# The opening of a fused LayerNorm, long-convolution and FFN kernel: warming products, tap products, the first weight load and early FFN blocks put in another order

## The chip, the cores and the metric

The kernel runs on one core of a Trainium2 chip. The metric is the device time of one execution in microseconds, as a median over several runs. Engines are named as in the profile: PE (TensorE matmuls; PEld its weight loads), DVE (VectorE), ACT (ScalarE), POOL (GpSimd), SP (SyncE, which issues most DMAs).

## The reference

```python
x = A_q                                   # 1 x 2048 x 640, bf16
xn = layernorm(x)
# branch s: a short causal convolution of k (4 taps), times v, then a convolution over all 2048 positions
k_shift = sum(k_pad[:, t:t + S, :] * shift_k[:, 3 - t] for t in range(4))
kv = k_shift * v
y = irfft(rfft(kv_pad) * rfft(ssm_k_pad))[:S] + kv * ssm_D
s = xn * y
# branch g: a feed-forward network, F = 1728
g = silu(gelu(xn @ w1 + b1) @ w2 + b2)
return x + s * g
```

## The kernel before, in words

Position p*16+j of the sequence lies in partition p, row j. The sixteen rows j are cut into four chunks of four (`xn_tiles`). The FFN takes one chunk (512 positions) at a time in transposed form: step `h` with number 14*c+ft multiplies 128 columns of `w1` (block ft of 14) with the five transposed tiles `xT` of chunk c, five products of 128x512 into one PSUM bank, and `he` takes the bank through Gelu on ACT (L400). `g` is the second product (28 half rows). The long convolution is a two-stage Fourier transform by matmuls: first stages `kf` (of the kernel) and `uf` (of the signal) with the matrices `WA` and `WB` (L351), small stages with 32x32 blocks, and their inverses. `WA` and `WB` are made in the kernel: DVE forms the integer phases (step `w`, L249), and ACT takes a Sin (`ws0`, L253), an Abs (`ws1`, L256), a second Sin (`ws2`, L258) and a small Sin (`ss`, L309). PSUM has eight banks, and `banks[:, b]` is one of them.

The order of the work is written out by hand: `prologue()` first, and then the text `PLAN`, whose entries name a step, its number, the engine of its copy (`.a` ACT, `.d` DVE, for stores `.s` SP and `.p` POOL) and, after `@`, the PSUM bank or the row slots in SBUF. Every engine and every DMA queue works through its own instructions in this order, and waits where an operand is not there or a bank or slot is still in use.

What `prologue()` does for chunk 0, in its order on each engine:

- SP: rows 0, 1 and 2-3 of chunk 0 (L665, three DMAs), then `w1` columns 0 to 640 (`load_w1(0)`, L208), and from `PLAN` the rest of `w1` (`A1`), `C0` and so on. `C0` to `C4` load `ssm_k` into rows 0 to 15 of `rows`; the four tap weights `skp` lie in row 12 to 15, in partition 0, until they are used.
- PE: `warm(6)`, six products of a zeroed 128x512 tile `blank` (L637); the tap products (`w_exp_matmuls`, L318), eight products of one row of ones with 320 strided elements, which spread the four taps over all partitions; the transposes of rows 0 and 1 (`turn(0)`, L646); `feed(ft, 0)` for ft = 0 to 4, the first 256 positions of five FFN blocks (25 products of 128x256, L391); the transposes of rows 2 and 3 (`turn(2)`); `feed(ft, 1)`, the second 256 positions of the five blocks (25 products); then `h9`, `pt` (a transpose of the biases), `h12`, `h7`, `h11` from `PLAN`.
- DVE: memsets, the integer product (L245), the statistics of the rows (L616, L619), the reciprocal (L625), the normalisation (L628), three of five copies of each `turn` (L153), and then `w`, the small phases `s`, statistics of the later chunks, and `pb`, which copies the biases out of PSUM (L529, L530).
- ACT: a Sqrt for the table (L668), two copies of zeros into `kh` (L674, L675), the roots (L622), the copies of the taps out of PSUM (`taps_out`, L640), two of five copies of each `turn` (L152), a Gelu for the table (L703), and then `ws0`, `ws1`, `ws2`, `ss` and the `he` of `PLAN`.

Blocks 0 to 4 lie in banks 0 to 4, `h9` in bank 5, the transposes and later `pt` and `h7` in bank 6, `h12` in bank 7; `h11` takes bank 1 after `he1`. `h5` stands in `PLAN` after `he8`.

Of the kernel before, what the change touches and what calls it, by code (L numbers as in the profile page):

```python
# [11 lines left out]
BF16 = mybir.dt.bfloat16  # L12
# [15 lines left out]
WARM0, WARM1 = 6, 0  # L28
EARLY = 5
# [9 lines left out]
ie2.a@98 kc5.d@100 kc12.a@101 kc4.d@102 kf3@2 ke3.a@104 lv1 lr1 cv0@106 cv5@16 he13 cv13@18 kt10@4 kf10@6 ln8
q3@20 ln11 ke10.a@22 g0@5 kf11@2 ge0@0 kf13@0 kf9@6 ke11.a ke13.a@24 kc10.d@103 ke9.a@26 g3@4 ln4 ge3@1 kf2@2  # L40
cv11@28 ln5 kf7@0 ke7.a ln6 ln7 tt6@5 V1@30 te6.a@32 tt5@6 tt7@7 te7.a@33 ks3.p cv3@34 kt13@4 kc13.a@73 ks5.s
te5.a@59 cv2 ln9 cv4 cv6 gm3 ke2.a ks1.p g6@0 kf12@4 ke12.a tt8@1 te8.a@60 ge6@2 kf8@6 cv7 cv25@62 kt15@2
kc15.a@61 cv9@76 ke8.a kt9@3 kc9.a@100 uf1@4 ue1.a@22 cv8@34 cv10 g2@1 ge2@3 uf3@6 q7@16 ue3.a@90 tt9@0 cv17@96
kf1@2 ks6.p ke1.a@104 uf0@4 g1@1 ue0.a cv12 cv14 V3@76 ln10 kf14@6 te9.a@80 ge1@1 ke14.a@28 kf0@2 ke0.a ks0.p
kt8@4 cv16@24 kc8.a@82 gm2 cv15 ks2.s V2@18 q1@88 cv21@30 kt11@5 kf15@0 kc11.a@75 V4@0 V6@2 ke15.a uf2@6 g7@2
ks7.p ue2.a V5@4 ks4.s fl4@6 uf7@3 ge7@3 tt11@5 te11.a@102 gm6 tt13@0 te13.a@85 uf6@6 ue6.a@8 ue7.a tt10@1
te10.a@92 g5@2 kf16@6 cv19@10 cv18 cv20 cv22 ge5@2 cv23 tt14@5 te14.a@12 uf5@3 uf11@0 ue5.a@14 ue11.a@106 g4@2
gm0 ke16.a@96 cv32@104 cv24@10 ge4@0 uf10@4 ue10.a h14@3 cv29@30 tt12@0 us3.p cv26 cv27@18 uf4@6 he14@13 uf9@1
gm5 fl0@28 cv28 h23@4 gm4 fl6@26 cv30 te12.d@72 h21@5 cv31 us1.p ue9.a@68 ue4.a uf14@0 he23@74 fl1@64 uf12@2
ue14.a@66 cv41@62 us2.s uf8@6 ue8.a cv37@8 ue12.a@34 h17@4 he17@81 uf15@0 ue15.a cv33@18 uf13@6 us7.s he21@83  # L50
tt19@2 te19.a@84 cv35@30 h18@3 ue13.d ff0@0+6 fe1.a@76 us4.s cv40@24 cv42 h22@4 cv43@90 us5.p he18@93 fl2@10
fe0.a kf24@6 h20@5 ke24.a@14 ff1@2+0 fe3.a@36 fe2.a cv57@38 cv34 cv53@106 h16@6 fl3@28 he16@94 kf17@0 ke17.a
h26@7 cv45@62 us6.p kf18@2 he22@66 h24@6 ke18.a@68 cv36 he20@67 cv38 ff2@0+2 cv39 fe4.a@64 cv48@18 fe5.a us0.p
cv49@40 mk0@42 ml0@30 he24@44 mk1@34 h19@4 cv50 uf16@0 h25@5 ue16.a@8 cv51@22 kf23@2 he19@82 ml1@10 he26@56
ke23.a@0 cv52 cv54 kf22@0 ke22.a mk2@40 ml4@46 ks8.p h15@6 he15@75 cv44 he25@45 ml2@22 h27@4 mu0@2+0 mp1@106
V7@32 mp0@30 he27 g8@7 ge8@2 gm8 kf19@5 ke19.a cv46 uf19@0 g9@4 ue19.a@90 cv55 fl5@96 mu1@2+6 ml6@42 kf25@0
ke25.a q0@76 mp3@62 ge9@0 g10@5 ge10@2 mc0@0+6 me1.a@10 mp2@2 fl7@100 kf28@4 ke28.a@30 ks11.p ks9.s me0.d ks12.p
kf20@2 ke20.d@106 uf17@6 ff3@0+4 ue17.a cv47 us8.s mu2@2+6 mp4@34 fe7.a@36 fe6.a ms0.s mk3@28 kf21@4 ke21.a
mp5@22 gm10 kf27@0 uf27@4 ke27.a@4 ue27.a@0 ff4@2+0 fe8.a@68 fe9.a ml3@14 cv59@6 ff5@4+6 fe11.a@40 fe10.a g11@2
ml7@64 ge11@2 gm9 ff6@0+6 fe13.a@8 cv56@96 cv58 fe12.d mk4@52 mc1@4+2 me3.d@10 me2.a kf29@6 ke29.a tt18@0 ks14.s  # L60
tt16@1 mk6@54 te18.d@59 mc2@4+2 me4.a@26 kf26@6 g12@0 ke26.a ks13.s mk5@38 cv60 ml5@2 cv61@62 cv62 gm11
te16.a@60 me5.a cv63 uf18@4 mu3@6+2 ge12@0 ue18.a g13@1 mp6@22 ge13@2 kf31@4 ke31.a@34 mp7@6 uf25@6 ue25.a@48
kf30@0 ke30.d mc3@2+4 me6.a@50 us9.p ks15.p ks10.s fl15@62 me7.d uf29@6 ue29.a@30 fl8@14 ms1.p uf20@0 ue20.d@104
uf22@2 fl9@32 ue22.a@4 uf30@4 ue30.a@28 uf23@6 ue23.a gm7 uf24@0 ue24.d tt15@2 h30@3 he30@80 us12.p gm13 fl10@36
te15.d@103 gm1 mu4@4+0 uf21@6 mp9@6 ue21.a mp8@22 g15@2 ge15@3 fl11@90 mu5@0+6 ms3.s g14@3 mp10@34 mp11@106
# [26 lines left out]
def kernel(  # L92
# [514 lines left out]
    def prologue():  # L607
# [23 lines left out]
        blank = rows[:, WE0, 0:4 * P]  # L631
        tp_of = [banks_b[:, 6 + t // 3, t % 3 * 2 * P:(t % 3 + 1) * 2 * P] for t in range(DT)]
        pw = banks[:, 7, :]

        def warm(n):
            for _ in range(n):
                nc.tensor.matmul(out=pw, lhsT=blank[:, 0:P], rhs=blank, start=True, stop=True)  # L637
# [19 lines left out]
        nc.vector.memset(blank, 0.0)  # L657
# [52 lines left out]
        for ft in range(EARLY):  # L710
            feed(ft, 1)
# [49 lines left out]
```

## Time and profile before

| | |
|---|---|
| median of 3 runs | 211.58 us (209.90, 212.39, 211.58) |
| the profiled execution | 212.68 us, of which the span of its instructions is 210.9 us |
| PE busy | 195.6 us (93%), 2176 matmuls |
| DVE busy | 175.9 us (83%) |
| ACT busy | 155.0 us (74%) |
| chain that ended last | PE 77%, ACT 10%, DMA 6% |
| DMA | 57.72 MB, mean 274 GB/s |

The profile is one execution of the program. Its times count from the first instruction of the span. A timeline row reads: start, busy time, engine, line, operation, output and input tiles with their shape, count, and in brackets the idle time of the engine before it and what ended it. A row can merge several instructions of one kind. PE rows include the time in which a product runs through the array; the distance of two starts is what one product costs in a row of them.

### The profile page before, as it was taken

The page shows a single profiled execution, that of the slowest core. Times are in us where ns is not written, and L with a number is a line of the kernel's source. Part 1 is how long each engine was busy: PE and PEld are TensorE (multiplying, and loading weights), DVE is VectorE, ACT ScalarE, POOL GpSimd, SP SyncE. Part 2 cuts the span into 40 slices and gives each one's busy share as a digit, 9 for nine tenths or more (in the row PEclk, how much of TensorE's full clock was granted, in tenths as well). Part 3 has the DMA queues.
Part 4 walks back from the last instruction along what each step waited for, and adds up shares of the span by engine and source line. Part 5 has one row for each costly group of instructions (what it writes and reads, how often), then busy time and mean ns, then how long its engine had stood idle before and what let it go on. Part 6 is the DMA issues. An engine that isn't in the chain of part 4 may idle for free.

```text
span 210.9 us, 5483 instructions
## 1 busy us (share of the span) xinstructions
PE 195.6 (93%) x2176; PEld 114.8 (54%) x2192; DVE 175.9 (83%) x307; ACT 155.0 (74%) x247; POOL 30.9 (15%) x55
## 2 busy tenths in 40 slices
PE   7698499999999999998899999999999989999992
PEld 2365157778776544563565644456655434357771
DVE  8829789999899999999999977762999888753894
ACT  6839959999999999969969899594144976753110
POOL 8100010403022021110012203100010100330330
PEclk9769859999999999999999999999999999999999
DMA  6999999715879899998868896757997678569963
GB/s 167 391 420 348 356 365 371 265 38 185 262 221 352 266 330 320 297 328 303 290 256 296 248 343 212 273 174 226 303 387 258 201 234 266 178 229 281 367 229 113
DMA packets 46876, 57.72 MB, mean 274 GB/s; under 512 B 3009, under 2 KB 36594, under 8 KB 46850
## 3 DMA queue, kind: packets, MB, share of 16 engines
q1 hardware_dynamic: 44016, 47.36, 68.6%
q0 software_dynamic: 2832, 10.00, 13.1%
q8 instruction: 17, 0.28, 0.5%
q14 instruction: 9, 0.07, 0.1%
q10 hardware_dynamic: 2, 0.01, 0.0%
HBM read 33.76 MB, written 18.35 MB: 247 GB/s over the span
## 4 chain that ended last, share of the span: by engine, by line
PE 77%; ACT 10%; DMA 6%; issue 3%; SPq 1%; DVE 1%; ACTq 0%
PE banks L391 28%; PE banks L413 26%; PE banks L351 8%; ACT rows L152 5%; PE banks L495 4%; PE banks L584 3%; DMA w_sb<-in_B_w_dram 3%; DMA rows<-rows 3%; PE banks L442 3%; PE banks L560 3%; PE banks L382 2%; PE banks L513 1%; ACT WB L253 1%; ACT WA L258 1%; ACT rows L256 1%
## 5 line engine op out<-in xcount | busy, mean ns | idle before, releaser
L391 PE MATMUL banks<-rows,w_sb 128*128 128x512 bf16 (+1 forms) x289 | 70.4, 382 | 7.3 <-ACT rows L400 1.9
L152 ACT CAST rows<-banks 128x640 bf16<-128x640 f32 x105 | 69.9, 720 | 4.0 <-PE banks L495 1.7
L413 PE MATMUL banks<-w_sb,rows 128*128 128x320 bf16 x416 | 61.7, 299 | 0.0
L549 DVE TENSOR_TENSOR rows<-banks,rows 128x1280 bf16<-128x1280 f32 x32 | 46.1, 1484 | 3.7 <-PE banks L495 2.5
L413 PEld LDWEIGHTS <-rows 128*128 128x128 bf16 x416 | 39.8, 98 | 16.8 <-issue 0.2
L391 PEld LDWEIGHTS <-w_sb 128*128 128x128 bf16 x305 | 29.6, 103 | 34.4 <-issue 8.3
L400 ACT ACTIVATE rows<-banks,b_f 128x512 bf16<-128x512 f32 x52 | 35.0, 704 | 9.8 <-PE banks L391 9.6
L418 ACT ACTIVATE sl_all<-banks 128x320 bf16<-128x320 f32 x32 | 14.5, 458 | 30.7 <-PE banks L413 28.5
L480 DVE TENSOR_TENSOR rows<-rows 128x1280 bf16<-128x1280 bf16 x32 | 26.1, 822 | 0.5
L476 DVE TENSOR_TENSOR rows<-rows 128x1280 bf16<-128x1280 bf16 x32 | 25.2, 820 | 0.8 <-DMA scrK<-rows 0.8
L153 DVE CAST rows<-banks 128x640 bf16<-128x640 f32 x23 | 18.6, 821 | 7.2 <-PE banks L560 3.9
L152 ACT COPY rows<-banks 128x512 bf16<-128x512 bf16 (+3 forms) x27 | 17.4, 695 | 4.0 <-PE banks L646 4.0
L351 PE MATMUL banks<-rows,WA 128*128 128x320 bf16 x64 | 18.7, 299 | 0.9 <-ACT rows L152 0.6
L351 PE MATMUL banks<-rows,WB 128*128 128x320 bf16 x64 | 18.7, 298 | 0.0
L423 DVE TENSOR_TENSOR xn<-xn,sl_all 128x320 bf16<-128x320 bf16 x32 | 10.0, 319 | 8.2 <-ACT sl_all L418 8.0
L495 PE MATMUL banks<-rows,mats 32*32 32x320 bf16 x512 | 12.9, 304 | 0.6 <-ACT rows L152 0.3
L596 DVE TENSOR_TENSOR rows<-banks,xn 128x640 bf16<-128x640 f32 x12 | 9.6, 819 | 2.8 <-PE banks L584 2.8
L495 PEld LDWEIGHTS <-mats 32*32 32x32 bf16 x512 | 5.2, 87 | 12.4 <-issue 10.7
L153 DVE COPY rows<-banks 128x640 bf16<-128x640 bf16 (+3 forms) x18 | 6.9, 411 | 4.8 <-PE banks L646 4.0
L584 PE MATMUL banks<-rows 128*128 128x320 bf16 x64 | 10.6, 299 | 0.1
L568 POOL DMA_DIRECT2D scrC<-rows x7 | 5.3, 764 | 36.5 <-ACT rows L152 28.0
L458 POOL DMA_DIRECT2D scrK<-rows x9 | 5.0, 553 | 36.4 <-ACT rows L152 32.2
(95 smaller groups left out, 182.2 us busy)
## 6 DMA issues: line engine op xcount, KB each, us to landing
rows<-scrK SPq DMA_DIRECT2D x16, 320.0 KB, 5.4
rows<-rows SPq DMA_DIRECT2D x32, 160.0 KB, 3.4
rows<-scrU SPq DMA_DIRECT2D x16, 320.0 KB, 5.0
rows<-scrC SPq DMA_DIRECT2D x16, 320.0 KB, 5.4
scrU<-rows POOLq DMA_DIRECT2D x10, 320.0 KB, 4.1
scrK<-rows POOLq DMA_DIRECT2D x9, 320.0 KB, 4.6
scrC<-rows SPq DMA_DIRECT2D x9, 320.0 KB, 3.5
rows<-in_A_ssm_k_dram SPq DMA_DIRECT2D x5, 512.0 KB, 11.9
```

The source lines that it names most:

```text
L152: return nc.scalar.copy(out=out_ap, in_=in_ap)
L153: return nc.vector.tensor_copy(out=out_ap, in_=in_ap)
L351: nc.tensor.matmul(out=ps[:, w, 0:HALF], lhsT=m[:, n, :], rhs=rhs, start=True, stop=True)
L391: nc.tensor.matmul(out=ps[:, cols], lhsT=w1_sb[:, t, ft * P:(ft + 1) * P], rhs=live["xT", c * DT + t][:, cols], start=(t == 0), stop=(t == ...
L400: nc.scalar.activation(out=o[0:M, 0:CH * P], in_=live["h", i][0:M, :], func=ACT.Gelu_apprx_tanh, bias=b1_f[0:M, ft:ft + 1], scale=1.0)
L413: nc.tensor.matmul(out=ps[:, 0:HALF], lhsT=live["hT", c * FT + ft][0:M, q * P:(q + 1) * P], rhs=w2_sb[0:M, ft, hs], start=(ft == 0), stop= ...
L418: nc.scalar.activation(out=live["sl", i], in_=live["g", i][:, 0:HALF], func=ACT.Silu)
L476: nc.vector.tensor_tensor(out=o, in0=kh[:, 3 + r - j:3 + r - j + KR, side(e)], in1=w_exp[:, j:j + 1, side(e)].to_broadcast([P, KR, HALF]), ...
L480: nc.vector.tensor_tensor(out=uc, in0=uc, in1=live["vc", i] if s == 7 else live["kv", x - 1], op=ALU.mult if s == 7 else ALU.add)
L495: nc.tensor.matmul(out=out[b][part(j)], lhsT=F2m[part(b), part(b)], rhs=pieces(src)[part(b), j, :], start=True, stop=True)
L549: nc.vector.tensor_tensor(out=p.rearrange("p k (h c) -> p k h c", h=2), in0=live["mu", g][:, None, :, 0:HALF].to_broadcast([P, 2, 2, HALF] ...
L584: nc.tensor.matmul(out=psY[:, u, 0:HALF], lhsT=live["G", 2 * w + n // 8][:, n % 8, :], rhs=cab[:, u, side(w)], start=(w == 0), stop=(w == 1))
```

## The change

`WARM0` goes from 6 to 12 and `EARLY` from 5 to 6 (six blocks are fed in the prologue, `h5` leaves `PLAN`). The warming products take the numbers of `r2` (the odd numbers of the phase product, read as bf16) in place of the zeroed tile, whose memset goes; they write bank 5. The four pairs of tap products and their copies move: taps 3 and 0 behind `turn(0)`, tap 1 behind the first and tap 2 behind the third `feed(ft, 1)`, both in banks 6 and 7. The first 768 columns of `w1` come in two parts: columns 0 to 384 ahead of rows 2-3 of chunk 0, columns 384 to 768 behind them. The two copies of zeros into `kh` become one activation with scale 0. In `PLAN` the order of the steps stays but for `h5`; only banks and slots are named anew, among them `h9@6`, `pt@7`, `h7@1`, `h11@0`, `it1@6`, `h6@0`.

```diff
-WARM0, WARM1 = 6, 0
-EARLY = 5
+WARM0 = 12
+EARLY = 6
...
-w A1 C0 ws0 s h9@5 X3 ws1 ws2 ss X2 ls11 pt@6 ls15 pb C2 he1@64 C1 sm d0 X1 ls14 ls13 ls12 K0 he0@65 he9@66
-he2@67 h12@7 ls9 C4 lv3 lr3 h7@6 h11@1 he11@68 it1@0 ie1.d@70 he7@69 he3@72 kt2@5 kc2.d@73 C3 ls4 h6@2 he6@74
+w A1 C0 ws0 s h9@6 X3 ws1 ws2 ss X2 ls11 pt@7 ls15 pb C2 he1@64 C1 sm d0 X1 ls14 ls13 ls12 K0 he0@65 he9@66
+he2@67 h12@7 ls9 C4 lv3 lr3 h7@1 h11@0 he11@68 it1@6 ie1.d@70 he7@69 he3@72 kt2@2 kc2.d@73 C3 ls4 h6@0 he6@74
...
     def load_w1(i):
-        a, b = ((0, EARLY * P), (EARLY * P, F))[i]
+        a, b = ((0, 3 * P), (EARLY * P, F), (3 * P, EARLY * P))[i]
...
-        blank = rows[:, WE0, 0:4 * P]
+        odd = r2.bitcast(BF16)
-        pw = banks[:, 7, :]
+        pw = banks[:, 5, :]
         def warm(n):
             for _ in range(n):
-                nc.tensor.matmul(out=pw, lhsT=blank[:, 0:P], rhs=blank, start=True, stop=True)
+                nc.tensor.matmul(out=pw.rearrange("p (a b) -> p a b", a=2), lhsT=odd[:, 0:P],
+                                 rhs=odd[:, None, :].to_broadcast([P, 2, 2 * P]), start=True, stop=True)
+        def taps(j, b):
+            psw[j] = w_exp_matmuls(j, b)
...
-        nc.vector.memset(blank, 0.0)
...
         for a, b in ((0, 1), (1, 2), (2, 4)):
+            if a == 2:
+                load_w1(0)
             nc.sync.dma_start(out=x0[:, a:b, :], in_=x_v[:, a:b, :])
-        load_w1(0)
+        load_w1(2)
...
-        nc.scalar.copy(out=kh[0:1, 0:3, 0:4 * P], in_=blank[0:1, None, :].to_broadcast([1, 3, 4 * P]))
-        nc.scalar.copy(out=kh[0:1, 0:3, 4 * P:D], in_=blank[0:1, None, 0:P].to_broadcast([1, 3, P]))
+        nc.scalar.activation(out=kh[0:1, 0:3, :].rearrange("o r (a b) -> o (r a) b", b=P),
+                             in_=odd[0:1, None, 0:P].to_broadcast([1, 3 * DT, P]), func=ACT.Copy, scale=0.0)
...
         warm(WARM0)
-        psw = {j: w_exp_matmuls(j, 2 * j) for j in (3, 0, 1, 2)}
-        warm(WARM1)
+        psw = {}
...
-        taps_out(3)
-        taps_out(0)
         rc(0)
...
         turn(0)
-        taps_out(1)
-        taps_out(2)
+        for j in (3, 0):
+            taps(j, 4 - 2 * (j == 0))
+            taps_out(j)
...
         for ft in range(EARLY):
             feed(ft, 1)
+            if ft in (0, 2):
+                j = 1 + ft // 2
+                taps(j, 6)
+                taps_out(j)
```

More of the change, by code (lines that the diff above doesn't have):

```diff
@@ L39 @@
[L39 to L53, printed above, removed]
@@ new lines @@
+he2@67 h12@7 ls9 C4 lv3 lr3 h7@1 h11@0 he11@68 it1@6 ie1.d@70 he7@69 he3@72 kt2@2 kc2.d@73 C3 ls4 h6@0 he6@74
+it0@6 kt3@1 ie0.a@108 ls5 ln15 B cv1@76 it3@2 ie3.a@78 kt6@3 ln12 ln14 kc6.a@75 kt1@0 kc1.d@80 K1 he4@81 ls10
+kc3.d@82 h8@6 he8@83 ls8 he5@84 kt0@2 kc0.a@85 q6@86 kf5@3 ke5.a@88 K2 K3 d1 V0@90 kt7@0 kc7.d@92 h10@6 lv2
+he12@93 kf4@1 ls6 it2@5 kt14@3 kt5@4 lr2 ln13 he10@94 ke4.a kc14.a@95 kt4@0 kf6@6 h13@1 ls7 kt12@2 ke6.a@96
+ie2.a@98 kc5.d@100 kc12.a@101 kc4.d@102 kf3@3 ke3.a@104 lv1 lr1 cv0@106 cv5@16 he13 cv13@18 kt10@6 kf10@2 ln8
@@ new lines @@
+kt8@6 cv16@18 kc8.a@82 gm2 cv15 ks2.s V2@24 q1@30 cv21@88 kt11@7 kf15@0 kc11.a@75 V4@0 V6@2 ke15.a uf2@2 g7@4
+ks7.p ue2.a V5@4 ks4.s fl4@6 uf7@5 ge7@3 tt11@7 te11.a@102 gm6 tt13@0 te13.a@85 uf6@2 ue6.a@8 ue7.a tt10@1
+te10.a@92 g5@4 kf16@2 cv19@10 cv18 cv20 cv22 ge5@2 cv23 tt14@7 te14.a@12 uf5@5 uf11@0 ue5.a@14 ue11.a@106 g4@4
+gm0 ke16.a@96 cv32@10 cv24@76 ge4@0 uf10@6 ue10.a h14@5 cv29@88 tt12@0 us3.p cv26 cv27@24 uf4@2 he14@13 uf9@6
+gm5 fl0@28 cv28 h23@1 gm4 fl6@62 cv30 te12.d@72 h21@4 cv31 us1.p ue9.a@26 ue4.a uf14@6 he23@74 fl1@68 uf12@2
@@ new lines @@
+ke23.a@0 cv52 cv54 kf22@6 ke22.a mk2@40 ml4@46 ks8.p h15@0 he15@75 cv44 he25@96 ml2@34 h27@5 mu0@2+6 mp1@106
+V7@32 mp0@88 he27 g8@1 ge8@2 gm8 kf19@4 ke19.a cv46 uf19@6 g9@0 ue19.a@18 cv55 fl5@22 mu1@2+4 ml6@42 kf25@6
+ke25.a q0@64 mp3@2 ge9@0 g10@1 ge10@2 mc0@6+4 me1.a@36 mp2@100 fl7@88 kf28@0 ke28.a@106 ks11.p ks9.s me0.d
+ks12.p kf20@2 ke20.d@66 uf17@4 ff3@6+0 ue17.a cv47 us8.s mu2@2+4 mp4@76 fe7.a@28 fe6.a ms0.s mk3@34 kf21@0
+ke21.a mp5@4 gm10 kf27@6 uf27@0 ke27.a@0 ue27.a@68 ff4@2+6 fe8.a@6 fe9.a ml3@38 cv59@40 ff5@0+4 fe11.a@26 fe10.a
@@ new lines @@
+te15.d@103 gm1 mu4@2+6 uf21@4 mp9@34 ue21.a mp8@58 g15@0 ge15@3 fl11@76 mu5@6+4 ms3.s g14@1 mp10@18 mp11@66
+mc4@2+6 me9.d@40 us10.p ge14@2 gm14 gm15 h31@0 tt17@1 te17.d@57 he31@73 me8.a us11.s h33@4 ff7@6+0 fe15.a@46
+fe14.d mk7@54 h35@5 he33@95 mc5@2+0 me11.d@104 me10.a he35@100 h32@6 he32@101 mu6@2+0 mp13@6 mp12@52 uf26@4
+ue26.a ms5.p h39@7 he39@13 uf28@4 ue28.a h40@6 he40@44 uf31@0 ue31.a mc6@4+2 me12.d@8 us14.p h29@7 me13.a
+he29@56 gm12 mu7@0+4 mp14@74 mp15@82 h36@6 he36@81 h37@2 h34@3 he34@93 ms2.s mc7@0+6 me14.d@34 h38@4 me15.a
@@ new lines @@
+he38@94 ff9@0+6 he37@96 fe18.d@58 fe19.a h28@5 he28@48 ff11@3+0 fe22.a@2 fe23.d h41@2 he41 ff8@6+0 fe16.d@26
+fe17.d ms6.s g16@5 us13.s ge16@1 gm16 g17@3 ms7.s ff10@6+0 g18@4 ge17@2 ms4.p yl2@88 yl3@50 gm17 fe20.a@18
+mk8@66 y2@2 yt2@49 us15.p ml8@38 fe21.a mk9@42 mu8@6+0 mp17@0 mp16@90 yl0@22 g19@5 ge18@3 gm18 yl4@62 y3@2
+yt3@104 y0@0 yt0@105 yo3@36 ml9@14 g21@4 ge19@0 ge21@1 mu9@6+2 fl12@6 g20@5 mp18@52 yl1@24 mp19@106 ge20@2 gm20
+mc8@0+6 me17.a@8 me16.a ml10@46 mk10@54 fl13@68 y4@4 yt4@37 mc9@2+6 me19.a@74 me18.d ys3.p y1@0 yl6@82 yt1@40
@@ new lines @@
+yl7@60 mu10@4+6 mp21@32 mp20@76 g23@2 ge23@3 gm23 ff13@0+6 fe26.d@34 fe27.a ml11@10 g22@3 ge22@2 mk11@28
+ff12@6+4 fe25.a@38 ml12@88 fl14@50 yo1@41 q2@22 gm19 gm21 fe24.a y6@0 mc10@2+4 yt6 mk12@66 yl5@26 mu11@6+0
+mp22@14 me21.a@0 me20.a h42@4 he42@85 mk13@42 y7@2 h43@5 ml13@90 mp23@58 mc11@6+0 he43@102 me23.a@62 me22.a gm22
+yt7 yo4@12 h46@4 he46@72 mu12@2+0 yo0@92 q4@52 h47@5 mp24@106 he47@104 ml14@24 mp25@46 h44@6 he44@36 ff14@2+4
+fe29.d@68 fe28.a mc12@0+6 me25.a@18 me24.a mk14@54 mu13@2+4 mp26@94 h45@6 ff15@0+2 fe31.a@100 fe30.a he45@13
@@ L88 @@
+yl15@90 y15@4 g30@6 ge30@0 yl10@0 y10@0 yt15 yo9@107 yt10@4 yo10@5 yl8@42 yo11@34 y8@2 g29@7 ge29@1 ys4.p gm30
+yl12@26 ga30 y12@4 ys0.p ys2.p ys10.s ys11.s yt8@35 gm29 gs25.p g31@6 gs30.s ga28 ga29 yt12@24 gs29.s yo8@25
+yo12@74 ys1.p ys8.s ys12.s ys13.p gs27.p ge31@2 gm31 ga31 gs31.s ys9.p
 """
```

57 lines of the change are left out of this document (20 added, 37 removed).

## The prediction

> **What bounds the kernel now.** I read the page first (busy shares and the forty slices), then the chain of waits up to 50 us, then the timeline of the first 36 us engine by engine, and last the windows that the granted clock draws.
>
> ```profile
> span 210.9 us, 5483 instructions
> PE 195.6 (93%) x2176; PEld 114.8 (54%) x2192; DVE 175.9 (83%) x307; ACT 155.0 (74%) x247; POOL 30.9 (15%) x55
> 31.40:93.00 61.60, 61.12 (x547) 40.53 (x551) 59.34 (x103) 60.27 (x101) 9.12 (x14) 1.00 0.83 267
> ```
>
> The third row is a window behind the opening: in 61.60 us PE is busy 61.12, DVE 59.34, ACT 60.27. All three are full, so what the opening loses on any of them has little room to come back. The opening itself hangs on another thread. The chain of waits:
>
> ```profile
> 2.12 6.61 DMA w_sb<-in_B_w_dram
> 8.77 5.51 PE banks L391 x25
> 14.28 0.61 PE banks L646 x10
> 14.92 0.65 ACT rows L152 x2
> 15.58 1.28 ACT L253
> 16.88 2.00 ACT WB L253
> ...
> 23.34 1.28 ACT L400
> 24.63 0.70 ACT rows L400
> 25.37 2.29 PE banks L391 x5
> ...
> 28.52 0.64 PE banks L442 x6
> ```
>
> The reader is to see that from 14.92 to 25.37 the chain is ACT alone: its copies of the second transposes, the Sin table, three sines and an Abs, the Gelu table, the first `he`. PE stands with eight groups of banks filled and can't go on before `he1` frees one at 25.33. So the opening is as long as the time until ACT can load the Sin table, 15.58, plus a fixed 9.79 us (25.37 - 15.58).
>
> The clock, in windows of 3.41 us that the trace itself shows as its steps:
>
> ```profile
> 0.58:3.99 3.41, 2.81 (x7) 0.86 (x8) 3.14 (x11) 2.71 (x3) 3.09 (x9) 1.00 0.58 164
> 4.00:7.40 3.40, 3.09 (x18) 1.23 (x16) 2.83 (x10) 2.03 (x6) 2.26 (x5) 1.00 1.00 324
> 7.41:10.82 3.41, 2.05 (x10) 1.49 (x11) 3.01 (x11) 3.12 (x6) 0.00 (x0) 0.50 1.04 406
> 10.82:14.22 3.40, 3.40 (x19) 2.41 (x17) 0.01 (x1) 0.48 (x2) 0.00 (x0) 0.50 1.04 428
> 21.06:24.46 3.40, 1.24 (x5) 0.48 (x5) 2.20 (x10) 3.38 (x3) 0.00 (x0) 1.00 0.98 337
> 24.48:27.88 3.40, 2.51 (x9) 1.11 (x9) 3.26 (x11) 2.75 (x6) 0.00 (x0) 0.50 1.03 376
> 27.88:31.29 3.41, 3.41 (x19) 2.01 (x18) 2.79 (x9) 1.67 (x3) 1.04 (x1) 0.50 1.08 367
> 205.38:208.79 3.41, 1.50 (x11) 0.85 (x9) 2.61 (x7) 0.44 (x1) 0.00 (x0) 1.00 0.49 159
> ```
>
> The first number behind the length is PE's busy time, the one before the DMA share the clock. The clock rose behind windows with PE busy 2.81 and 3.40 us, not behind 2.05 and 2.51; it held behind 1.50 and fell behind 1.24. Behind 4.00 to 7.40 it fell although PE counts 3.09 busy: most of that was one-row tap products, which seemingly count for nothing. (The record begins at 3.99; the 1.00 of the first row is no reading, the products there ran at half rate, below.) So all 25 first feeds ran at half clock, and so did the restart from 25.37 to 31.29.
>
> **The change, part by part.** Prices and places in the opening:
>
> ```profile
> 2.01 0.15 PEld L637 LDWEIGHTS <-rows 128*128 128x128 bf16 x1 [0.28 <-issue]
> 2.44 0.15 PEld L637 LDWEIGHTS <-rows 128*128 128x128 bf16 x1 [0.28 <-issue]
> 4.40 0.11 PEld L318 LDWEIGHTS <-ones 1*128 1x128 bf16 x1 [0.17 <-issue]
> 4.69 0.11 PEld L318 LDWEIGHTS <-ones 1*128 1x128 bf16 x1 [0.17 <-issue]
> 5.71 1.27 ACT L640 CAST rows<-banks 128x640 bf16<-128x640 f32 x2
> 6.54 0.81 PE L646 MATMUL banks<-ident,xn 128*128 128x128 bf16 x10 [0.26 <-DVE xn L628]
> 6.75 0.49 DVE L616 BATCH_NORM_STATS2 stats<-xn 128x6 f32<-128x320 bf16 x1
> 7.35 0.69 DVE L153 COPY rows<-banks 128x256 bf16<-128x256 bf16 x3
> 10.03 0.80 DVE L628 TENSOR_SCALAR xn<-xn,mv,rstd 128x640 bf16<-128x640 bf16 x2
> L391 PE MATMUL banks<-rows,w_sb 128*128 128x256 bf16 x21 | 2.5, 272 | 0.0
> 14.92 0.65 ACT L152 COPY rows<-banks 128x256 bf16<-128x256 bf16 x2 [3.60 <-PE banks L646]
> 15.09 1.85 SPq L211 DMA_DIRECT2D rows<-in_A_ssm_k_dram  x2
> 15.41 1.22 DVE L249 TENSOR_SCALAR rows<-rows 128x2048 int32<-128x2048 int32 x1
> 27.70 1.85 ACT L400 ACTIVATE rows<-banks,b_f 128x512 bf16<-128x512 f32 x3 [0.64 <-PE banks L391]
> 28.62 1.13 DVE L153 COPY rows<-banks 128x1024 bf16<-128x1024 bf16 x2 [0.59 <-PE banks L513]
> 31.33 0.69 ACT L400 ACTIVATE rows<-banks,b_f 128x512 bf16<-128x512 f32 x1 [1.78 <-PE banks L391]
> w_sb<-in_B_w_dram SPq DMA_DIRECT2D x1, 800.0 KB, 6.6
> ```
>
> *Warming.* A 512-wide product costs 0.43 at half clock (2.44 - 2.01), so 0.215 at full. Twelve from 1.2 us on, with the clock rising at 4.0, end near 5.2; never rising, near 6.3. Both lie ahead of the transposes at 6.5, so the products themselves cost nothing. In the window to 7.40 they leave about 1.2 us busy and the transposes 0.8: 2.0, over the 1.50 that held. I take the clock as full from 4.0 on. The dropped memset and the merged zero copies save DVE and ACT some 0.1 to 0.2 us, in slack on ACT and at most 0.1 on DVE's way to the transposes; I take 0.1.
>
> *Taps 3 and 0 behind the first transposes.* Four products at 0.285 (4.69 - 4.40) are 1.14 us of PE: transposes issued by 7.1, taps until 8.25. That covers DVE's and ACT's copies of the transposes (DVE's end at 8.04 = 7.35 + 0.69, and much the same after the change); without the cover the feeds could start 0.25 earlier.
>
> *w1 in two parts.* Before, 1440 KB (x and the first part) had landed at 2.12 + 6.61 = 8.72. Now the first 480 KB stand behind 320 KB of x: at the same pace 2.0 + 6.7 x 800/1440 = 5.7; rows 2-3 by 7.2 (1120 KB), the second part by 9.4 (1600 KB), against its first reader at about 9.9. Rows 2-3 are read at 6.75 by DVE, ahead of its copies of the transposes, so DVE may wait 0.4 us there and the feeds by up to 0.3; bounds 0 and 0.3, I take 0, as the estimate is loose by more. On SP one DMA more stands in the queue, and `C4`, `C3` and the w2 loads behind them now wait until the last tap products have read the tap weights, about 15.6 instead of 15.09: the DMA share is 1.04 up to 14.22 with earlier loads still in the queue, so 0, and 0.5 at most. POOL's instructions stay.
>
> *Feeds.* At full clock a feed product costs (2.5 - 0.27)/20 = 0.11. Thirty from 8.25 take 3.3 and end at 11.55; before, 25 at half clock ended at 14.1. The normalised rows 2-3 are there at 10.83. Transposes and copies as before (14.1 to 15.57): ACT's copies end at 13.0 instead of 15.57. **Term 1: -2.57.**
>
> *Taps 1 and 2 on ACT's path.* The Sin table is loaded behind both copies. Counted from the end T of ACT's transposes' copies: the first second-half feed ends at about T + 0.3 (an estimate: its last two products need ACT's copies, two at 0.11 and a start), the taps take until T + 0.87, the copy starts 0.2 later and takes 0.65 (1.27/2); PE goes on with two feeds, 10 x 0.11, to T + 1.96, second taps to T + 2.53, copy to about T + 3.45. Before, the table load followed at T + 0.02. **Term 2: +3.43.** Were the strided taps half as dear, it would be +2.9. DVE's phase (1.22 us, at T) is long done, so it hides nothing. The Sin table thus loads at 16.45 and PE restarts at 26.24: the opening comes out 0.87 later, not earlier.
>
> *Six early blocks.* PSUM has eight banks, and in both kernels eight groups are computed before `he1`: before, h0 to h4, h9, h12, h7; now h0 to h5, h9, h12. `h5` is needed only by the late `he5`; its bank is blocked, and `h7` moves behind the restart, ahead of `h11`. Five 512-wide products cost 2.13 at half clock and half of that at full. So `he11`, which ACT did at 27.70, waits for two groups: 26.24 + 4.27 + 0.25 = 30.75; DVE's copy at 28.62 comes at about 31.45 (+2.8), and the `he6` of 31.33 at about 33.0 (+1.7), the clock rising at 31.29 as before. Where `h5` stood PE gets 1.08 back. **Term 3: +0.4 on PE, +1.7 on ACT, +2.8 on DVE by about 36 us, the 0.87 included.** Behind it the three engines are as full as the first window shows, so the end lies between; I take ACT's, since it is busy without a gap there and is the middle one.
>
> *Sum.* The profiled execution took 212.68 (span 210.9), 1.1 over the median of 211.58; with 1.7 it is 214.4. In it the clock rose about as late as it can both times. If the windows lie at random, the feeds of before end on average 0.7 earlier and term 1 shrinks to -1.85, for a total near 2.4. On the median that gives 213.3 to 214.0; I say **213.6**, 1.0% more.
>
> **A rule of the skill.** The Trainium skill, "TensorE: Matmul & The Clock Gate", Part 4, says that transposes don't count as busy for the clock gate. By it the window to 7.40 would hold only the 1.2 to 1.4 us of warming, between the 1.24 that fell and the 1.50 that held, and the second rival below would be the likely case; the rise behind 27.88 to 31.29, of which transposes (the chain's L442 at 28.52) held 0.64 and more, speaks against it. The same page, Part 1, has the window of 3.4 us free-running, which no single profile shows; by it the runs of one kernel would differ.
>
> **The rivals.**
> - *Faster: the tap copies don't hold up the Sin.* If ACT loaded the Sin table by T + 0.5, term 1 alone would count: 211.58 - 2.57 = 209.0. For it speaks only that ACT idles 3.60 us ahead of those copies; against it the order of ACT's work, in which the taps stand ahead of the sines. Chance 0.10.
> - *The clock falls again before the feeds.* Then the feeds start at half clock and are full from 10.82 (+1.25) or not at all (+3.1): 214.8 to 216.7. The 1.24 that fell is near. Chance 0.20.
> - *The lag is absorbed, the change does nothing.* ACT and DVE catch up in gaps behind 78 us (1.2 and 0.9 of ACT in the row below), and PE's 0.4 is left: 212.0. Against it: the few gaps. Chance 0.25.
>
> ```profile
> ACT rows L152 <- PE banks L351: 1.2, 1, 1.2
> ACT sl_all L418 <- PE banks L413: 0.9, 1, 0.9
> ```
>
> **How the numbers follow.** The forecast has 0.45, half of it on either side of +1% (213.7). About 1% is what a measurement of this kernel can tell from no change. Faster: 0.10. Slower: 0.23 + 0.20 = 0.43. Same: 0.22 + 0.25 = 0.47. The range leaves out the first rival and the upper half of the second, and goes as far below the third's 212.0 as the runs of before spread about their middle (1.2): 210.8 to 215.9.
>
> **What would show it.** Feeds at 0.11 apart from the first one on, ending near 11.6: term 1. The Sin table load near 16.5, with two casts and PE's waits ahead of it: term 2. Ten products between the restart and `he11`, and ACT idle for over 2 us there: term 3. Wrong it would be if the load stood ahead of the casts, if the clock read 0.50 at 9 us, or if PE's restart came before 25.

## The result and the profile after

The changed kernel takes 218.4 us (median of 217.4, 218.2, 218.6 and 220.0), the kernel before 211.0 in the same session: ratio 1.035, 95% interval 1.026 to 1.045. It is slower, by more than the range allowed (215.9). The profiled execution took 217.4, span 215.6, against 212.68 and 210.9: +4.7 between the two profiles, +7.4 between the medians. Here and below a ratio leaves out runs over 1.5% above the fastest of the same kernel (with the kernel before, all of these have a mean granted clock of 0.984 or less), so means over all runs stand beside it.

The chain of the profile after, which answers to the chain shown before:

```profile
8.48 3.61 PE banks L391 x30
12.09 0.46 PE banks L650 x8
...
12.92 0.88 PE banks L391 x5
13.80 0.65 PE banks L318 x2
14.45 1.20 PE banks L391 x10
15.65 0.67 PE banks L318 x2
...
16.34 0.69 ACT rows L644
...
17.05 1.28 ACT L253
...
26.09 0.70 ACT rows L400
...
26.83 4.43 PE banks L391 x10
```

The thirty feeds run 0.11 apart (only the first two steps are 0.19 and 0.20), and their phase ends at 12.09 where the first 25 ended at about 14.1 before. Then the chain goes through the taps (L318, the copy L644), which were not on it before. The Sin table (L253) loads at 17.05 instead of 15.58. From there to the restart it is 9.78, as before (9.79).

The timeline of the profile after, first ACT, then DVE:

```profile
12.68 0.65 ACT L152 COPY rows<-banks 128x256 bf16<-128x256 bf16 x2 [0.59 <-PE banks L650]
14.49 0.69 ACT L644 CAST rows<-banks 128x640 bf16<-128x640 f32 x1 [1.16 <-DVE rows L278]
16.34 0.69 ACT L644 CAST rows<-banks 128x640 bf16<-128x640 f32 x1 [1.16 <-PE banks L318]
31.29 1.84 ACT L400 ACTIVATE rows<-banks,b_f 128x512 bf16<-128x512 f32 x3 [2.78 <-PE banks L391]
33.46 0.69 ACT L400 ACTIVATE rows<-banks,b_f 128x512 bf16<-128x512 f32 x1 [0.32 <-PE banks L391]
96.74 0.69 ACT L152 CAST rows<-banks 128x640 bf16<-128x640 f32 x1 [1.17 <-PE banks L351]
```
```profile
7.74 0.49 DVE L616 BATCH_NORM_STATS2 stats<-xn 128x6 f32<-128x320 bf16 x1 [0.99 <-DMA xn<-in_A_q_dram]
32.07 1.09 DVE L153 COPY rows<-banks 128x1024 bf16<-128x1024 bf16 x2 [2.58 <-ACT rows L400]
62.69 0.83 DVE L476 TENSOR_TENSOR rows<-rows 128x1280 bf16<-128x1280 bf16 x1 [1.87 <-DMA scrK<-rows]
```

Each tap copy costs its 0.69 and a wait of 1.16. (The first wait is put down to a DVE row that happened to end then; what that copy reads are PE's tap products, started at 13.80 in the chain.) `he11` comes at 31.29, behind ten products (3.59 later than the 27.70 of before), DVE's copy at 32.07 (+3.45), `he6` at 33.46 (+2.13). The lag doesn't settle at ACT's: the row at 96.74 is 3.55 later than its counterpart before, and the span ends 4.7 later. The counterpart has the same idle time ahead of it:

```profile
93.19 0.69 ACT L152 CAST rows<-banks 128x640 bf16<-128x640 f32 x1 [1.16 <-PE banks L351]
```

How the lag grows behind the restart is seen on PE, first a row of before, then two of after:

```profile
35.39 0.55 PE L442 MATMUL banks<-ident,rows 128*128 128x128 bf16 x6
```
```profile
36.35 0.53 PE L442 MATMUL banks<-ident,rows 128*128 128x128 bf16 x6
37.20 0.30 PE L351 MATMUL banks<-rows,WB 128*128 128x320 bf16 x1 [0.18 <-ACT rows L400]
```

Where `h5` is left out PE catches up, and is 0.96 late at 36.35, against the forecast's 0.4. But then it waits for ACT, which is about 2 us late: 0.18 here, and 0.15, 0.23 and 0.30 up to 44.57. The row at 44.71 (41.98 before) is 2.73 late. In return ACT waits 0.41 for PE at 49.53, and is 2.4 to 2.7 late from there to 65 us.

The windows of the profile after (length, PE's busy time, ..., then the granted clock ahead of the DMA share):

```profile
4.37:7.78 3.41, 2.48 (x19) 1.12 (x17) 1.96 (x8) 0.86 (x4) 1.85 (x4) 1.00 1.06 369
7.78:11.19 3.41, 3.41 (x27) 2.40 (x26) 3.01 (x12) 2.34 (x5) 0.00 (x0) 1.00 1.06 408
21.43:24.85 3.42, 0.00 (x0) 0.00 (x0) 0.04 (x1) 3.37 (x4) 0.00 (x0) 1.00 1.01 360
28.26:31.68 3.42, 3.42 (x14) 1.51 (x12) 1.20 (x5) 0.64 (x2) 1.04 (x1) 0.50 1.10 360
31.68:93.00 61.32, 59.18 (x518) 38.80 (x522) 58.32 (x104) 59.29 (x101) 9.12 (x14) 1.00 0.74 246
```

The clock stays full through the feeds. In the stall PE does nothing for a whole window, and the restart runs at half clock until 31.68. In the stretch behind, PE idles 2.14 us (0.48 in the window shown before), DVE and ACT 0.7 more than before.

### The profile page after: what moved, and what is told of

Read it like the earlier page. It is cut to its first block, busy times and chain, and to the rows that moved or that the text cites. A ratio compares the mean times of both kernels' runs of the same rounds, so it can differ in the third digit from the quotient of the medians.

```text
span 215.6 us, 5504 instructions
## 1 busy us (share of the span) xinstructions
PE 195.1 (90%) x2187; PEld 113.6 (53%) x2203; DVE 175.5 (81%) x306; ACT 155.2 (72%) x246; POOL 30.8 (14%) x55
## 4 chain that ended last, share of the span: by engine, by line
PE 61%; ACT 17%; DVE 11%; DMA 5%; issue 5%; POOL 0%; ACTq 0%; SPq 0%; DVEq 0%; POOLq 0%
PE banks L391 24%; PE banks L413 19%; ACT rows L152 10%; PE banks L351 4%; PE banks L584 4%; PE banks L560 3%; PE banks L495 3%; DVE rows L480 3%; DVE rows L549 2%; DVE rows L476 2%; DMA rows<-scrC 2%; ACT rows L400 2%; DMA scrK<-rows 2%; PE banks L318 1%; DMA scrC<-rows 1%
## 5 line engine op out<-in xcount | busy, mean ns | idle before, releaser
L391 PE MATMUL banks<-rows,w_sb 128*128 128x512 bf16 (+1 forms) x294 | 68.1, 366 | 8.6 <-ACT rows L400 5.6
L391 PEld LDWEIGHTS <-w_sb 128*128 128x128 bf16 x310 | 28.8, 99 | 35.9 <-issue 13.1
L468 POOL DMA_DIRECT2D scrU<-rows x10 | 5.4, 542 | 34.8 <-ACT rows L152 30.6
L361 DVE BATCH_NORM_STATS2 st<-xn 128x6 f32<-128x320 bf16 x24 | 10.3, 472 | 0.0
```

Of the source, the lines that this page charges most:

```text
L391: nc.tensor.matmul(out=ps[:, cols], lhsT=w1_sb[:, t, ft * P:(ft + 1) * P], rhs=live["xT", c * DT + t][:, cols], start=(t == 0), stop=(t == ...
```

## The experiments

My theory after the result: the opening came as forecast, and the lag behind it is set by three things that the forecast had too small or not at all, `h5` in the place of `h7`, the renamed slots, and the clock at the restart. Rivals were that the late tap copies do all of it, that DVE's lag alone decides, and that the clock is the same in both kernels. The expectations state the theories as they stood when each run was planned; theory D is the one on the clock.

One thing has to be known for all that follows. The mean granted clock of a run counts the time ahead of its first recorded change as full, as the prediction noted for one row. e10's profile (a kernel below without warming products) shows what that hides: its clock rises at 11.97 for the first time, and the feeds up to there stand 0.21 apart, half speed. The window ahead of that rise reads 1.00 all the same, and the run's mean is 1.000:

```profile
8.55:11.97 3.42, 3.42 (x17) 2.24 (x16) 2.15 (x8) 2.90 (x5) 0.00 (x0) 1.00 1.04 400
```

So a mean of 1.0 says that the clock did not fall, not that it rose early.

**One part at a time (e1 to e4).** e1 puts all four tap products behind the first transposes again, e2 keeps the late taps but feeds five blocks with the plan and slots of before, e3 does both, e4 is the opening of before with the six blocks and the plan of the change.

```diff
 e1, e3:
-        for j in (3, 0):
+        for j in (3, 0, 1, 2):
...
-            if ft in (0, 2):
 e2, e3:  (and PLAN of before)
-EARLY = 6
+EARLY = 5
 e4, against before:  (and PLAN of after)
-EARLY = 5
+EARLY = 6
```

> The changed kernel, with taps 1 and 2 put right behind the first transposes with the other two, so that no tap copy stands between the second transposes and the Sin table. Theory A (two losses in the opening, the tap copies on ACT and h7 behind the restart, each carried to the end and somewhat enlarged by DVE): Sin table at about 14.3 in place of 17.05, restart near 24.1, time about 215. Theory B (the newly named banks and slots of the plan make waits later on): Sin table early, but 217.5 to 218.5. Theory C (only the exchange of h5 for h7 costs): no better than 217.

> The changed kernel with five early blocks and the plan of before, banks and slots included; taps 1 and 2 stay behind the second feeds. Theory A: Sin table near 16.5, restart near 26.2, but he11 no more than 1.5 later than before (27.7) and DVE's copy of the WA transposes no more than 1.5 later (28.6); time about 213. Theory B: 211 to 211.5, as the later waits are gone. Theory C: 211 or less.

> Both edits: warm products, taps all behind the first transposes, five early blocks, the plan of before. Theory A: Sin table near 13.7, nearly 2 us ahead of before, and time about 209.5. Theories B and C: the early Sin table doesn't decide, 211.

> The kernel before with six early blocks and the plan of the changed kernel alone: the taps, the warming products and the order of loads stay as before (the first w1 load is 768 columns wide). Theory A: Sin table 1 to 1.5 later than 15.58, since a sixth block is fed at half clock, h7 behind the restart: time about 214. Theory B: 217 to 218.5, nearly the whole loss. Theory C: 217 or more as well, with the loss seen at he11 and not later.

| kernel | median us | ratio to before, interval | mean of all runs (before 210.84) |
|---|---|---|---|
| e1 | 215.65 | 1.020, 1.009 to 1.031 | 215.90 |
| e2 | 213.72 | 1.014, 1.005 to 1.023 | 213.97 |
| e3 | 212.55 | 1.000, 0.994 to 1.007 | 212.03 |
| e4 | 216.38 | 1.025, 1.017 to 1.033 | 216.35 |

The six blocks with their plan cost 5.5 us without the new opening (e4, between the 214 of theory A and the 217 of theory B). That is more than the late taps cost with five blocks (1.9 by the means, 2.8 by the ratios, e2 less e3). So the rival that the tap copies do all of it fell. e2 came as theory A had it (Sin table 16.53, `he11` 28.64). e3 missed: expected at 209.5 with the Sin table at 13.7, it is as fast as before, and in its profile the table loads at 15.36, since the clock fell from 10.88 to 14.29. e1 is no clean reading of the taps either: in its profile the clock fell from 8.46 to 15.28, and the Sin table loaded at 17.03, as late as with the late taps. Two of its other runs, at a granted clock of 0.984, take 214.3 and 214.4, near the 215 of theory A.

**Does DVE's lag decide (e5)?** DVE's copy of `it1` and `kt2` is put ahead of `h7` and `h11` in the changed kernel.

```diff
-h7@1 h11@0 he11@68 it1@6 ie1.d@70 he7@69 he3@72 kt2@2 kc2.d@73
+it1@6 ie1.d@70 kt2@2 kc2.d@73 h7@1 h11@0 he11@68 he7@69 he3@72
```

> The changed kernel with the transposes of WA and of the kernel rows (it1, kt2 and their DVE copies) put ahead of h7 and h11 in the plan. Theory A (DVE's lag of 3.4 behind the restart is the largest and is what the end follows): DVE's first copy of 1024 comes near 28.5 in place of 32.07, DVE's lag falls under ACT's, and the time falls by 1 to 2, to about 217. Rival (ACT's lag decides): ACT waits one microsecond longer for he11, the time is 218.5 to 219.5.

220.78 us, ratio 1.047 (1.037 to 1.056). DVE's copy came 1.2 earlier than after (30.88), `he11` 2.7 later:

```profile
30.88 1.08 DVE L153 COPY rows<-banks 128x1024 bf16<-128x1024 bf16 x2
```
```profile
33.95 1.84 ACT L400 ACTIVATE rows<-banks,b_f 128x512 bf16<-128x512 f32 x3 [3.96 <-PE banks L391]
```

The time is above both expectations. DVE's lag alone doesn't decide; the theory fell. The run isn't clean either: this execution lost its clock in the opening, which is that of the changed kernel, and its Sin table loaded at 18.52, which is 1.5 of the 2.7.

```profile
4.97:8.39 3.42, 2.79 (x18) 1.09 (x16) 1.87 (x8) 1.39 (x4) 1.24 (x3) 1.00 1.07 381
8.39:11.80 3.41, 3.32 (x17) 2.30 (x17) 2.91 (x11) 2.25 (x4) 0.00 (x0) 0.50 1.06 411
```

The window to 8.39 caught 0.3 us less of the warming than that of the profile after, and more of the one-row tap products. So the forecast's rival of a clock that falls before the feeds does occur in some executions.

**The renamed slots (e6, e9).** e6 is the kernel before with the 192 changed SBUF slots of the new plan and nothing else; e9 is the changed kernel with the slots of before (its lines stand three lower in the profile).

```diff
 e6, against before (one of 192 places):
-V2@18 q1@88 cv21@30
+V2@24 q1@30 cv21@88
 e9: the same places the other way, in the changed kernel
```

> The kernel before with the SBUF row slots of the changed plan alone (192 entries), banks, opening and order as before. Theory B in its small form (the new slots make a copy wait for a store that still reads its slot, 0.7 near 100 us, as the trace of the six-block kernel shows): time 0.5 to 1.0 over before. If slots cost nothing: within 0.3 of before. If they are the main loss: 214 or more.

> The changed kernel with the SBUF row slots of the plan of before (192 entries back); opening, six blocks and banks as changed. Theory B small (the new slots cost about 3 us, as in the kernel before with the new slots): about 215.5, DVE's gap at the copy that waited 1.87 for a store of scrK gone. Rival (the slots only matter where the opening is as before, or hide behind the opening's delay): 218.

e6: 214.33, ratio 1.016 (1.006 to 1.025); mean 214.13 against 211.29, more than the 0.5 to 1.0 us that I had expected. No instruction is other than before, only where a row of `rows` lies, and so which load or store must end before a slot is filled again. In e6 the waits stand near 100 us (lines lower than before's), and the clock falls behind them:

```profile
101.80 0.50 PE L442 MATMUL banks<-rows,mats 32*32 32x320 bf16 x16 [2.15 <-DMA rows<-rows]
```
```profile
102.73 0.83 DVE L423 TENSOR_TENSOR rows<-rows 128x1280 bf16<-128x1280 bf16 x1 [1.33 <-DMA scrC<-rows]
```
```profile
97.95:101.36 3.41, 1.38 (x20) 0.52 (x20) 3.41 (x5) 1.60 (x4) 0.00 (x0) 1.00 0.97 350
101.36:104.77 3.41, 2.88 (x26) 1.56 (x26) 1.70 (x3) 2.77 (x5) 0.00 (x0) 0.50 0.82 225
```

The profile after has its counterpart at the same place:

```profile
104.72 0.36 PE L495 MATMUL banks<-rows,mats 32*32 32x320 bf16 x16 [0.82 <-ACT rows L152]
```

This wait of PE is 0.82 to 2.15 in all six profiles with the new slots (after, e1, e4, e5, e6, e8) and 0.26 to 0.27 in all eleven with the old ones, six blocks (e9, e11) or five.

e9: 216.38, ratio 1.0345 (1.0293 to 1.0398); mean 216.39, between the 215.5 and the 218 of the expectation. The span is 214.6, 1.0 less than after. The two ratios, 1.035 each, can't be compared: the one of the changed kernel takes in runs of before with a lower clock, and against all runs of before e9 stands at 1.027. The mean of the changed kernel is 2.2 higher than e9's (218.55, in another session, where before was 0.5 higher); the granted clock of its four runs is 0.984 to 0.965, of e9's 0.984 to 0.980, so a part of the 2.2 is clock, at most some 1.5 (0.007 of 216 us).

**The clock at the restart (e8, e12, and two more profiles of before).** e8 puts 22 products that nobody reads ahead of `h12` in the changed kernel, e12 nine ahead of `h7` in the kernel before, so that PE isn't idle in the stall.

```diff
+    def keep(n):
+        for _ in range(n):
+            nc.tensor.matmul(out=banks[:, 7, :], lhsT=w1_sb[:, 0, 0:P], rhs=live["xT", 0][:, 0:4 * P],
+                             start=True, stop=True)
 e8:  (in e12 bank 6)
-he2@67 h12@7
+he2@67 k22 h12@7
 e12:
-lv3 lr3 h7@6
+lv3 lr3 k9 h7@6
```

> The kernel before, unchanged, for a second profile. Theory D (the kernel before often keeps the full clock over its opening's gap, since h7 at 22.24 splits PE's idle time, while the changed kernel with 5.6 us without a matmul never does): in this profile the granted clock stays 1.00 at 25 us, the five products of h11 take about 1.2 in place of 2.29, and the time is about 210. Rival: the clock falls at 24.5 as in the first profile, and the restart of before is always at half clock.

> The changed kernel with 22 products of 128x512 more, into bank 7, between the bias transposes and h12, whose results nobody reads: PE then has no gap over 1.5 us before the restart. Theory D: the granted clock stays 1.00, h7 and h11 take 2.2 in place of 4.43, he11 starts near 29.1 in place of 31.29, and the time falls by 2 to 2.5, to about 216. Rival (the restart's rate is hidden behind ACT): 218 as before.

> The kernel before, unchanged, for one more profile. Theory D (its times fall into two groups by whether the clock falls in the stall ahead of the restart): with this execution's granted clock at .985 or more, the restart at 25.4 us runs at full clock, the first ten products of the restart take about 2.2 us, not 4.4, and the span is about 208; at a lower clock it looks as in the two profiles so far (span 211 to 212). Rival: the lower-clock executions lose elsewhere (near 100 us), and the restart is at half clock in all of them.

> The kernel before with nine products that nobody reads put ahead of its h7, so that TensorE isn't empty in the stall before the restart. Theory D: the restart is at full clock in every execution, all times lie in the faster group of before (about 209.8 us, ratio about 0.995), and its granted clock is .985 or more in each run. Rival: the restart is bound by ACT's eviction pace and not by the clock, then the ratio is 1.00 and the spread stays as it is.

e8: 216.66, ratio 1.027 (1.016 to 1.037); mean 216.49, 2.1 below the changed kernel, granted clock 0.988 to 1.0 in its runs. Its restart, `h7` and `h11`, answers to the ten products at 26.83 in the chain of after:

```profile
26.60 2.32 PE L391 MATMUL banks<-rows,w_sb 128*128 128x512 bf16 x10 [0.82 <-ACT rows L400]
```

They take 2.32 instead of 4.43, and `he11` comes at 28.95 (expected 29.1). e12: 210.04, ratio 1.004 (0.999 to 1.008); mean 210.23 against 210.41. Both more profiles of before (times 213.87 and 212.96; median of ten runs 212.14, ratio 1.001, 0.995 to 1.007) had the restart at half clock, like the first. First the rows of before's third profile, then e12's:

```profile
19.43:22.84 3.41, 1.27 (x6) 0.48 (x5) 2.18 (x10) 3.36 (x4) 0.00 (x0) 1.00 1.00 292
22.84:26.25 3.41, 2.02 (x5) 0.71 (x5) 3.31 (x12) 3.06 (x5) 0.00 (x0) 0.50 1.01 394
```
```profile
17.92:21.33 3.41, 1.77 (x10) 0.71 (x8) 2.18 (x10) 3.36 (x4) 0.00 (x0) 1.00 1.06 326
21.33:24.74 3.41, 3.41 (x21) 1.65 (x20) 3.34 (x10) 3.40 (x5) 0.00 (x0) 1.00 0.99 324
```

PE busy 1.27 in a window of the stall let the clock fall, 1.77 held it. Over 78 runs of before, 45 have a granted clock of 0.985 or more, with a mean of 209.8; the other 33 have 212.5. (One fall of 6.8 us at half clock in 211 takes 0.016.) All twelve runs of e12 are at 0.987 or more, so the filled stall keeps the clock. None of the 45 was profiled: that they keep the clock at the restart follows from e12, and was not seen. And e12's mean of 210.2 is not their 209.8; three of its runs reach 211.4 to 211.9 at a clock of 1.0. So e12 gained nothing by the ratio that I expected at 0.995. What the second spread comes from stays open. It may still be the clock: at a mean of 1.0 its first rise can have come late, as at 12.61 and 13.54 in before's third and second profile.

**Tap copies on DVE (e7, e10, e11, e13).** e7 is the new opening with five blocks, before's plan and slots, and taps 1 and 2 copied by DVE behind `w`, so that ACT goes from its transposes to the Sin table. e10 is e7 without warming products; e11 is e7 with six blocks and the changed order; e13 is e7 with eight unread products (`k8`, as above) ahead of `h12`.

```diff
-                taps_out(j)
+                if ft == 0:
+                    f1_phase()
+                nc.vector.tensor_copy(out=halves(w_exp[:, j, :]), in_=psw[j][:, :, 0:HALF])
```

> The changed opening with five blocks and the plan of before, where taps 1 and 2 are copied out of PSUM by DVE, behind the phase of the sines, in place of ACT. Theory A (the opening is as long as the way to the Sin table): Sin table at about 12.3 in place of 15.58, restart near 22.1, time 207 to 208. Rival (something else, as the loads or DVE, is next in line and gives it back): 209.5 to 211.

> The same kernel as the one with the copies on DVE, with no warming product at all. If the warming products are what brings full clock to the feeds: first feeds 0.21 apart, Sin table about 2.5 later than with them, time 2 to 2.5 over it. If the transposes and feeds reach full clock as early without: no difference.

> The changed kernel with six blocks, copies of taps 1 and 2 on DVE and the slots of before: what is left against the five-block kernel of this call is h5 taking h7's place ahead of the restart and five products more in the opening. Theory A: 1.5 to 2.5 over the five-block kernel, he11 two groups behind the restart. Rival (the exchange costs nothing once the rest is mended): the same time within 0.5.

> The changed opening with five early blocks, before's order and slots, taps 1 and 2 copied by DVE, and eight products that nobody reads put ahead of its h12. If the clock is what takes back the lead of the earlier Sin table load: about 208.5 to 209.5 us, ratio .985 to .995. Rival: the lead is given back at the waits on stores to the scratch between 76 and 160 us whatever the clock does: about 210.3 again, ratio 1.00 to 1.01.

The four came out as follows: e7 has the Sin table at 12.57 (expected 12.3), but its time is the rival's; e10 is 1.4 over e7 (expected 2 to 2.5); e11 is 2.9 over it (expected 1.5 to 2.5); e13 is in the rival's range by its ratio. Three of them (e13 aside), with e9 and the changed kernel, make a ladder, in which each row differs from the one above by one edit. With the six blocks go the PSUM banks, which the plan names anew throughout; no run separates the two.

| kernel | ratio to before, interval | mean of all runs | span of its profile |
|---|---|---|---|
| e10: no warming | 1.0135, 1.0088 to 1.0182 | 211.98 | 209.5 |
| e7: with warming | 1.0063, 1.0024 to 1.0102 | 210.55 | 208.3 |
| e11: six blocks, banks | 1.0205, 1.0136 to 1.0273 | 213.44 | 211.8 |
| e9: tap copies on ACT | 1.0345, 1.0293 to 1.0398 | 216.39 | 214.6 |
| changed: new slots | 1.0354, 1.0262 to 1.0446 | 218.55 | 215.6 |

Before itself has a mean of 210.62 in the session of the first four. Warming gains 1.4, six blocks with their banks cost 2.9, the copies on ACT 2.95, the slots about 1 (1.0 by the profiles, 1.7 by the means less the difference of the sessions, a part of it clock). e13: 209.41, ratio 1.003 (0.998 to 1.007); mean 209.90 against 210.41. It is the fastest median of all (before 210.16), but no measured gain.

e7 has the Sin table 3.0 earlier than the profile of before, and yet its time is before's:

```profile
12.57 1.28 ACT L253 ACT_TABLE_LOAD   x1
```
```profile
13.56 1.28 ACT L253 ACT_TABLE_LOAD   x1
```

The second row is e12's, whose opening is that of before: with the clock risen at 11.1 its Sin table loads at 13.56; in before's three profiles at 15.58, 15.21 and 14.45. Against that opening the lead is 1.0. And DVE, which now copies the taps ahead of its small phases, comes to its 128x1024 copy at 26.45 in e13 against 25.91 in e12.

How six blocks lose time is seen in the profiles of e7 and e11, which both lost the clock for one window at the restart, and whose spans differ by 3.4. `he11` comes 1.74 later in e11 (27.65 against 25.91). The same table load of ACT, first in e7, then in e11 (whose lines stand three lower), is 3.13 later:

```profile
64.46 1.28 ACT L400 ACT_TABLE_LOAD   x1
```
```profile
67.59 1.28 ACT L397 ACT_TABLE_LOAD   x1
```

So most of the loss is there by then. It grew as in the profile after, by PE waiting for ACT's copies between 40 and 41 us (0.35 and 0.30) and ACT for PE at 45.7 (0.41), and by a wait of ACT of 0.67 for a store at 55 us. Then DVE and PE wait:

```profile
64.93 2.29 DVE L473 TENSOR_TENSOR rows<-rows 128x1280 bf16<-128x1280 bf16 x3 [1.91 <-DMA scrK<-rows]
```
```profile
71.76 0.31 PE L348 MATMUL banks<-rows,WA 128*128 128x320 bf16 x1 [0.96 <-DVE rows L477]
```

DVE waits 1.91 for a store to the scratch, and then PE 0.96 for DVE. ACT is 4.2 late behind it, and 3.6 again by 78 us, so little of this pair remains at the end. e7 has no wait of 0.4 or more of either kind at this place; e9 has 1.47, after 1.87. But before's second profile had 2.08 there and its first 0.75, so what sets this wait is only partly the change; it was not taken apart.

## Why the prediction was wrong

*Term 1, and the clock in the opening: right but for the size.* ACT's copies of the second transposes end at 13.33 against 13.0. DVE waited 0.99 for rows 2-3 where I had set 0 and 0.3 at most; the feeds started 0.23 late (8.48) and cost the 0.11 forecast, but for the first two. Warming is worth 1.4 (e7 against e10). Measured from the typical run, though, term 1 is smaller than either -2.57 or the -1.85 put on the median: the five profiles with before's opening (its own three, e6 and e12) load the Sin table at 14.65 on average, 1.3 behind 13.33.

*Term 2: right.* From those copies to the Sin table it took 3.72 against 3.45 (3.38, if the steps given there are added up); the opening came out 1.46 later on the profiles against 0.87. In the time the two copies cost 2.95 (e9 against e11).

*Term 3: the step that failed.* The places came as forecast, each 0.5 to 0.6 late from the terms ahead of it: `he11` 31.29 (30.75), the DVE copy 32.07 (31.45), `he6` 33.46 (33.0). The failed sentence is "so the end lies between; I take ACT's", which makes the swap of `h5` and `h7` worth 0.83 net (1.7 - 0.87). Alone, with its banks, it costs 2.9 (e11 against e7), of which 0.54 is the sixth block's feeds in the opening, costed in term 1. ACT and DVE waited 2.78 and 2.58 at the restart (0.64 and 0.59 before). The lag then did not settle between the engines but was handed on: PE got the time of `h5` back (0.96 late at 36.35) and lost it to ACT's late copies (2.73 at 44.71), ACT lost 0.8 to PE in turn (1.85 late at 47 us, 2.63 at 52), and the store wait of 62.69, with PE waiting for DVE behind it, took ACT from 2.55 at 65 us to 3.55 at 97. Nor was e5's reading right that DVE decides. The gaps of ACT at 93 and 95 us that a rival of mine wanted to use as slack are still there (1.17 at 96.74): PE ends them, and PE is late as well.

*Left out: the slots.* The part by part costing says nothing of the renamed slots. They cost 1.3% (means) to 1.6% (ratio) alone in e6, a second fall of the clock included, and about 1 us in the changed kernel (e9).

*Taken as given: the clock at the restart.* I read the half-clock restart of the one profile as that of both kernels. Before shows a granted clock of 0.985 or more in 45 of 78 runs; none of the changed kernel's four has 0.985, as one window of its stall has no product at all, and filling the stall gives back 2.1 (e8). The Trainium skill, "TensorE: Matmul & The Clock Gate", Part 1, calls the window free-running; the runs agree: in before's three profiles the same opening meets the clock's steps at other places (first rise at 3.99, 13.54 and 12.61), and its runs fall into two groups 2.8 us apart. I had cited it and used it for the first feeds, and not for the restart.

In sum, on the profiles: 217.4 against the 214.4 worked out there, 3.0 short, of which the opening is 0.6, the lag from there to 97 us 1.25 (3.55 less 1.7 and 0.6), and the wait near 105 us and the rest up to the end 1.15 (4.7 less 3.55). The further 2.7 between the medians is 1.7 by which the profile of before lay over its median and 1.0 by which the one of after lay under its own. The clock goes the same way (0.968 in the former, 0.984 in the latter against 0.965 to 0.976 in the other three), but that it is all of the 2.7 is not shown. Of the rivals, the faster one fell on its price as well: e7 makes its condition true and takes 210.3, not 209.0.

## What to carry to other kernels

Before putting a copy into an in-order engine's queue, look at what stands behind it: two copies of 0.7 us ahead of a table load cost 3 us, since each also waits for its producer. When a block is computed early, ask which one it puts late, and follow the late one to all its readers; and cost renamed buffers as an edit of their own. Where a stall of PE is about as long as a clock window, compare several runs' granted clocks before taking one profile's restart as the kernel's, and look in the profile when the clock first rose, which the mean doesn't tell.

## What was not expected of the hardware

The first products of the profile after, and a window of e8 with the one behind it:

```profile
1.22 4.30 PE L637 MATMUL banks<-rows 128*128 128x512 bf16 x12 [1.22 <-POOL rows L242]
6.45 0.81 PE L650 MATMUL banks<-ident,xn 128*128 128x128 bf16 x10 [0.93 <-DVE xn L628]
```
```profile
98.17:101.58 3.41, 1.88 (x36) 0.80 (x23) 3.41 (x5) 2.59 (x5) 0.00 (x0) 1.00 1.05 371
101.58:104.99 3.41, 3.09 (x26) 1.68 (x26) 2.48 (x4) 2.55 (x5) 0.00 (x0) 0.50 0.98 302
```

- One-row products seem to hold no clock. In e3 a window (7.46 to 10.88) with 1.34 us of feeds and 2.15 of one-row taps let it fall; in e5 one with 0.85 of warming, 0.81 of transposes and 1.21 of taps did so too, while the window of the profile after from 4.37, with 1.15, 0.81 and 0.59, held it. 1.15 alone is less than the 1.27 and the 1.34 that fell elsewhere, so the transposes seem to count here, by a margin of about 0.2 us, and not in full (0.85 and 0.81 fell, where 1.50 of whole-array products held). The Trainium skill, "TensorE: Matmul & The Clock Gate", Part 4, says of the transpose mode that "it doesn't count as PE-busy the same way". Counting in part agrees with that; not counting at all, as I had read it, does not agree with the runs.
- 32-row products seem to count little too: e8 lost its clock at 101.58 behind a window with PE busy 1.88, thirty of whose 36 products had 32 rows, while e12's stall held it with 1.77 of whole-array products.
